# A gated mix of two linear attentions: one key-value piece issued earlier, another lock slack in the planner, one scaling on POOL, other merge orders

## The chip, the core and the metric

The kernel runs on one core of one Trainium2 chip. The core has five engines that work side by side, each through its own list of instructions in order: TensorE (PE, matrix products into PSUM; its weight loads are shown as PEld), VectorE (DVE), ScalarE (ACT), GpSimd (POOL) and SyncE (SP), which here issues the DMA transfers. They wait for each other through semaphores. The metric is the device time of one execution in microseconds; lower is better.

## The reference, cut to what matters

Two attention blocks over the same input `x` (2048 rows of 576, 32 heads of 18), mixed by a gate for each row. All data is float32.

```python
x = A_x
g = _sigmoid((x * gate_w).sum(-1, keepdims=True))
a = _A_ref(x, A_wqkv, A_wo)            # features: where(t > 0, t + 1, exp(t)) + 1e-6
b = _B_ref(x, B_wqkv, B_w_phi, B_wo)   # features: softmax(t @ w_phi) and softmax(-t @ w_phi)
return g * a + (1 - g) * b

# in each block, with feature maps pq and pk:
kv = jnp.einsum("bhsd,bhse->bhde", pk, v)
z = jnp.einsum("bhsd->bhd", pk)
num = jnp.einsum("bhqd,bhde->bhqe", pq, kv)
den = jnp.einsum("bhqd,bhd->bhq", pq, z)[..., None] + 1e-6
o = num / den                          # then (all heads side by side) @ wo
```

## The kernel before

**Three passes.** `S` is cut into 16 tiles of 128 rows, taken in eight pairs. The first pass (to about 139 us) forms keys and values of block A and sums `pk` by `v` into PSUM in key-value pieces (`kv_a`). The second (to about 273 us) does the same for block B (`kv_b`). The third makes the queries of both blocks at once, divides, transposes, multiplies by the summed key-values and by the output weights, and writes the result. Its first part, to about 350 us, is a start-up in which the first pairs come into flow; from 364 us on it repeats a block of some 34 us for each pair.

**The products.** A pair's products are one Strassen step: `strassen` makes seven products in seven units (i = 0 to 6), each a run of matmuls of 128x288 on high and low parts of an operand, into PSUM tiles named `X`, `Y` and `Z` in the code and `tr`, `pq` or `bk` in the profile. Between the units ScalarE copies a partial sum out (`keep`, shown as `row<-tr` and the like) and VectorE adds (`row<-row,pq`, `vo<-row,pq`), and TensorE may go on in that PSUM tile only when they have read it.

**The second pass.** A loop over n = 0 to 7 runs the seven units of pair n. In unit 6 it issues the key-value piece of the pair before: `kv_b(done)`, 64 matmuls of `vo` (values) by `uw`, `at` or `st` (the softmaxed keys), 19x36 each, as one piece that the planner doesn't divide. The profile records each of these float32 matmuls twice, so a piece shows as 128 records. The keys come out of `softmax_exp` (a row's maximum and minimum on VectorE, `mm`; differences; one exponential on ScalarE; the sums `ss` and their reciprocals `rs` on VectorE) and `scale_uw`, on POOL here (`uw<-uw,rs`). `steps(prep)` puts the preparation of the third pass's weights between the units: their high parts on ScalarE, the remainders on VectorE or POOL, and stores to memory (`wq<-at`, `wod<-op`).

**The third pass.** `q_units` is `strassen` with the query weights. `norm_a` and `norm_b` divide a tile by its denominators. In `norm_b` the two products of `uw` and `z_b` are on POOL and VectorE, the sums over heads (`dd<-row`) on VectorE, and then `dd<-dd,rs`, `den<-dd`, a reciprocal, `rs<-den,gate,rs` and `scale_ub` (`late<-uw,rs`). `tr_units` transposes the results (`tr<-ident,late`, `tr<-ident,row`), `num` multiplies by the key-values (`tr<-uT,kb`, `bk<-uT,kb`) and `out_units` by the output weights (`bk<-op,vo`, `bk<-op,at`). `merge` interleaves the units of these three in one list, each list with a weight and an offset: unit k of n stands at offset + weight (k + 0.5) / n.

**What sets the order.** Nothing is emitted as it is written. Every operation is recorded in a `Plan`, with a cost from `weigh` and, from `order`, a due time: for TensorE its place in the written order, for the others the due time of what needs them. `run` then simulates the engines and at each step gives an engine the operation with the earliest due time among those that could start soon. Most elementwise operations of VectorE and POOL on SBUF tiles carry `op.lock`: the planner holds that they don't overlap. `lock` is the planned end of the last such operation, and one on the other engine may start a slack before it (line 310). The order that comes out is what `emit` writes, so all instructions show line 360.

Of the kernel before, what the change touches and what calls it, by code (L numbers as in the profile page):

```python
# [15 lines left out]
ALU = mybir.AluOpType  # L16
# [131 lines left out]
class Plan:  # L148
# [128 lines left out]
    def run(self, tags):  # L277
        ops = self.ops
        for op in ops:
            op.left, op.est = len(op.deps), 0  # L280
        free = {e: 800 for e in ("PE", "ACT", "DVE", "POOL", "SP")}
        ready = {e: [] for e in free}
        slots = {tag: [0] * ts[0].bufs for tag, ts in tags.items()}
        pend = {tag: list(ts) for tag, ts in tags.items()}
        started, last, left = set(), {}, {t: t.ops for ts in tags.values() for t in ts}
        for op in ops:
            if not op.left:
                ready[op.eng].append(op)
        lock, dma, mode = 0, 0, False
        out = []  # L290
        SL = {"PE": 120, "ACT": 250, "DVE": 250, "POOL": 100, "SP": 50}
        while len(out) < len(ops):
            best = None
            for e, ops_e in ready.items():
                cand = []
                for op in ops_e:
                    s = max(free[e], op.est)
                    taken = {}
                    for t in op.tiles:
                        if t not in started:  # L300
                            free_at = sorted(slots[t.tag])
                            k = taken[t.tag] = taken.get(t.tag, -1) + 1
                            if pend[t.tag].index(t) >= len(free_at):
                                s = None
                                break
                            s = max(s, free_at[k])
                    if s is None:
                        continue
                    if op.lock:
                        s = max(s, lock - (220 if e == "POOL" else 30))  # L310
                    cand.append((s, op, 110 if e == "PE" and op.mode != mode else 0))
                if not cand:
                    continue
                first = min(s for s, _, _ in cand)
                due, _, s, op = min((op.due + 2 * turn, op.i, s + turn, op) for s, op, turn in cand if s <= first + SL[e])
                if best is None or s < best[0]:
                    best = (s, e, op)
            s, e, op = best
            ready[e].remove(op)
            for t in op.tiles:  # L320
                if t not in started:
                    started.add(t)
                    pend[t.tag].remove(t)
                    slots[t.tag].remove(min(slots[t.tag]))
            end = s + op.cost
            free[e] = end
            if op.dma:
                dma = max(s + 1000, dma) + op.dma / 370
                end = dma + 750
            elif e == "PE":  # L330
                mode = op.mode
            if op.lock:
                lock = end
            if not op.dma:
                end += op.lag
            op.key = s
            out.append(op)
            for t in op.tiles:
                left[t] -= 1
                last[t] = max(last.get(t, 0), end + self.SEM)  # L340
                if not left[t]:
                    slots[t.tag].append(last[t])
            for i in op.succ:
                o = ops[i]
                o.left -= 1
                o.est = max(o.est, end + self.SEM if o.eng != e or op.dma else end + 30 if e in ("DVE", "ACT") else free[e])
                if not o.left:
                    ready[o.eng].append(o)
        self.span = max(free.values())
        return out  # L350
# [14 lines left out]
def tile_gated_mix(ctx, tc, xT, wAk, wAv, wBv, wAq, wkT, wqT, phi, woA, woB, out):  # L365
# [382 lines left out]
    def kv_a(pend):  # L748
        with plan.piece():
            for t, f in pend:  # L750
                for gr, nh in kv_order(t):
                    p, a = side(t, gr)
                    kv_group(t, 3 * gr, nh, kv[0][64 * a:64 * a + VC * nh, 54 * p:54 * p + DH * nh],
                             f[:, 54 * gr:54 * gr + DH * nh], p == 0)

    def kv_b(pend):
        with plan.piece():
            for t, uw in pend:
                for j in range(QH):
                    for q, nh in QUADS:  # L760
                        if j < nh:
                            h = QH * q + j
                            kv_group(t, h, 1, kv[1][32 * q:32 * q + VC, 36 * j:36 * j + 36].rearrange("p (s d) -> p s d", s=2),
                                     uw[:, :, DH * h:DH * h + DH], j == 0)
# [20 lines left out]
    x = x_plain(0, raw)  # L785
# [60 lines left out]
    x = x_plain(1, raw)  # L846
# [203 lines left out]
    for n in range(NT // 2):  # L1050
        done, pend = pend, []
        if n % 2:
            lo = wk.tile([P, 2, D], F32, name="st", bufs=1) if n == 1 else area[0][:, :2 * D].rearrange("p (s n) -> p s n", s=2)
            uws = [lo, area[1][:, 896:].rearrange("p (s n) -> p s n", s=2)]
        else:
            uws = [uw_tile(), uw_tile()]
        for i, _ in enumerate(strassen(x, WB, TB, HB, two_banks, lambda: uws[0][:, 0], *b_sinks(n, uws, pend))):
            if i == 2 and n < 2:
                x_next = x_prep(n, raw, sums if n == 0 else sums[:2] + [chunks(row_tile()[:, :3 * P])])
                if n == 0:  # L1060
                    x_load_raw(1, raw)
            if i == 3 and 1 < n < NT // 2 - 1:
                x_next = x_fetch(n)
            if i == 6:
                if n:
                    kv_b(done)
                else:
                    kv_a(a_done)
            if n + i > 3:
                steps(prep)  # L1070
            if n == NT // 2 - 1 and i == 2:
                join_out()
        x = x_next
# [68 lines left out]
    def norm_b(t, uw, rs, ub, engs):  # L1142
        dd = sm.tile([P, 64], F32, name="dd")
        for s in range(2):
            zw = row_tile()[:, :D]
            engs[s].tensor_tensor(zw, uw[:, s, :], z_b[:, s], op=ALU.mult)
            V.tensor_reduce(dd[:, 32 * s:32 * s + 32], zw.rearrange("p (h d) -> p h d", d=DH),
                            op=ALU.add, axis=AX.X)
        V.tensor_tensor(dd, dd, rs, op=ALU.mult)
        den = sm.tile([P, 32], F32, name="den")  # L1150
        V.scalar_tensor_tensor(den, dd[:, :32], EPS, dd[:, 32:], op0=ALU.add, op1=ALU.add)
        V.reciprocal(den, den)
        r2 = rs.rearrange("p (s h) -> p s h", s=2)
        V.scalar_tensor_tensor(r2, den[:, None, :].to_broadcast([P, 2, 32]), gate[:, 1, at_row(t):at_row(t) + 1], r2, op0=ALU.mult, op1=ALU.mult)
        scale_ub(ub, uw, rs, engs[2])
# [115 lines left out]
    def chain(*gens):  # L1271
        for g in gens:
            yield from g
# [11 lines left out]
    for i in range(NT // 2 + 1):  # L1285
        while norms:
            norms.pop(0)()
        cur, prev = blocks[i], blocks[i - 1]
        seqs = []
        if i and i <= NT // 2:  # L1290
            prev["ot"] = num(uT, prev["at"], i >= NT // 2 - 1)
        if i + 1 < NT // 2:
            x = x_fetch(pairs[i + 1])
            if i == 0:
                load_out(3, x["dma"])
                load_out(4, x["dma"])
            if i == 1:
                for k, m in enumerate((1, 4, 6)):
                    load_out(k, x["dma"][m:m + 1])
            uws = [extra_uw, wk.tile([P, 2, D], F32, name="st", bufs=1)] if i == 0 else [uw_tile(), uw_tile()]  # L1300
            seqs.append((7, (0.4, 0) if i == 0 else (0.5, 0) if i == 1 else .7, q_units(i + 1, x, uws, row_tile)))
        ts = (2 * i + 1, 2 * i)
        if i < NT // 2:
            at = at_tile([2, 4, 256], F32R)
            cur["at"] = (at[:, 0], at[:, 1])
            seqs.append((8, (1, 0) if i == 0 else (0.7, 0.3) if i == 1 else 1, chain(*[tr_units(t, cur["at"], uT) for t in ts])))
        if i:
            seqs.append((4, (1, 0) if i == 1 else 1, chain(*[out_units(t, prev) for t in (2 * i - 1, 2 * i - 2)])))
        merge(*seqs)
    plan.emit(tc)  # L1310

# [89 lines left out]
```

## Time and profile before

| | us |
|---|---|
| three runs | 554.77, 556.88, 558.15 |
| their median | 556.88 |
| the profiled execution | 560.84 |
| its span (first to last instruction) | 559.1 |
| TensorE idle within the span, 559.1 - 544.7 | 14.4 |
| mean granted clock of TensorE | 0.994 |

The profile is of one execution, at 560.84 us somewhat above the three runs. In its rows `out<-in` are the program's tile names with the numbers left out, then the form, the type and how many (x). A time in square brackets is how long the engine stood idle ahead of the row, with what released it. "Issue" there means that the engine waited for nothing that the profile shows. The granted clock is the share of full speed at which TensorE was let run.

### The profile page before, as it was taken

Reading aid. Unit: us, or ns where it says so; the run is one execution under the profiler, and the core shown is the slowest. Engines: PE = TensorE matmul, PEld = TensorE weight load, DVE = VectorE, ACT = ScalarE, POOL = GpSimd, SP = SyncE. Lnnn points to the kernel's source line nnn. Section 1 sums busy time; section 2 is a strip of 40 time slices with the busy share of each in tenths; the row PEclk is TensorE's granted clock in tenths of the full one; section 3 lists DMA queues with packets and bytes.
Section 4 is the critical chain, followed back from the end, with each engine's and each line's share of the span. In section 5 each row is a group of like instructions: output and inputs, shape, how many; then the busy total and the mean of one; then the engine's idle time right before and its main releaser. Section 6 shows DMA issues by size and latency. Waiting matters only on the chain.

```text
span 559.1 us, 12938 instructions
## 1 busy us (share of the span) xinstructions
PE 544.7 (97%) x5233; PEld 524.7 (94%) x5233; DVE 411.5 (74%) x622; ACT 291.8 (52%) x613; POOL 252.8 (45%) x223
## 2 busy tenths in 40 slices
PE   8999998999999999999898999999999999999997
PEld 8999998999999989999898889999999999999997
DVE  5883568843698698989669999759688695976910
ACT  6665685654654545444265745445454544535521
POOL 6784396540885335354328666215243241523100
PEclk9999998999999999999899999999999999999999
DMA  8639756869578857659766921232321313100001
GB/s 283 256 130 306 263 198 244 302 232 364 186 295 290 263 197 261 200 194 333 240 189 201 366 90 51 69 106 70 105 80 59 110 54 109 68 2 23 34 32 42
DMA packets 39872, 96.38 MB, mean 172 GB/s; under 512 B 5440, under 2 KB 9024, under 8 KB 38276
## 3 DMA queue, kind: packets, MB, share of 16 engines
q1 hardware_dynamic: 39812, 95.56, 49.7%
q8 instruction: 41, 0.67, 0.5%
q14 instruction: 19, 0.16, 0.1%
HBM read 59.64 MB, written 36.70 MB: 172 GB/s over the span
## 4 chain that ended last, share of the span: by engine, by line
PE 87%; DVE 5%; ACT 2%; DMA 2%; POOL 2%; issue 2%; SPq 0%; DVEq 0%; ACTq 0%; POOLq 0%
PE pq L360 37%; PE bk L360 25%; PE tr L360 25%; ACT row L360 1%; POOL late L360 1%; DMA at<-wqT 1%; DVE at L360 1%; DVE row L360 1%; POOL row L360 1%; DVE dd L360 1%; DMA at<-xT 1%; DVE vo L360 1%; ACT op L360 0%; DMA xu<-x0x 0%; DVE st L360 0%
## 5 line engine op out<-in xcount | busy, mean ns | idle before, releaser
L360 PE MATMUL pq<-op,x 128*128 128x288 f32 (+1 forms) x636 | 105.7, 301 | 0.7 <-DVE vo L360 0.7
L360 PEld LDWEIGHTS pq<-op,x 128*128 128x128 f32 x636 | 92.1, 191 | 1.7 <-DVE vo L360 0.9
L360 PE MATMUL bk<-op,vo 128*128 128x288 f32 x480 | 70.5, 296 | 0.0
L360 PE MATMUL pq<-tail,x 128*128 128x288 f32 (+1 forms) x308 | 66.5, 300 | 0.0
L360 PEld LDWEIGHTS bk<-op,vo 128*128 128x128 f32 x480 | 65.7, 188 | 0.1
L360 POOL TENSOR_TENSOR row<-row,z_a 128x576 f32<-128x576 f32 x16 | 25.0, 1565 | 78.7 <-DVE row L360 68.4
L360 PE MATMUL pq<-op,xp 128*128 128x288 f32 (+1 forms) x336 | 53.4, 297 | 0.5 <-ACT row L360 0.5
L360 PE MATMUL bk<-op,at 128*128 128x288 f32 x288 | 51.4, 302 | 0.0
L360 ACT ACTIVATE row<-tr 128x288 f32<-128x288 f32 (+1 forms) x74 | 30.0, 407 | 38.1 <-PE tr L360 37.6
L360 PEld LDWEIGHTS pq<-tail,x 128*128 128x128 f32 x308 | 49.3, 190 | 0.6 <-DVE row L360 0.2
L360 ACT ACTIVATE row<-bk 128x288 f32<-128x288 f32 (+3 forms) x43 | 17.5, 410 | 60.5 <-PE bk L360 60.4
L360 PEld LDWEIGHTS pq<-op,xp 128*128 128x128 f32 x336 | 47.5, 188 | 0.7 <-ACT row L360 0.7
L360 ACT ACTIVATE row<-row,epsc 128x576 f32<-128x576 f32 x54 | 41.9, 776 | 7.1 <-DVE row L360 6.3
L360 DVE TENSOR_REDUCE ss<-uw 128x64 f32<-128x1152 f32 x22 | 29.6, 1347 | 20.9 <-ACT uw L360 20.8
L360 DVE TENSOR_TENSOR row<-row,pq 128x576 f32<-128x576 f32 (+1 forms) x30 | 22.4, 747 | 29.1 <-PE pq L360 14.0
L360 POOL TENSOR_TENSOR x<-at,x 128x384 fp32r<-128x384 f32 (+2 forms) x35 | 33.7, 963 | 21.8 <-ACT x L360 21.8
L360 PEld LDWEIGHTS bk<-op,at 128*128 128x128 f32 x288 | 41.8, 189 | 0.4 <-issue 0.4
L360 POOL TENSOR_TENSOR row<-row,den 128x378 f32<-128x378 f32 (+1 forms) x32 | 22.3, 715 | 31.8 <-DVE den L360 29.4
L360 PE MATMUL tr<-op,xv 128*128 128x288 f32 (+1 forms) x204 | 33.6, 302 | 0.0
L360 PE MATMUL tr<-op,xu 128*128 128x288 f32 (+1 forms) x192 | 31.1, 314 | 2.1 <-DVE row L360 2.1
L360 ACT ACTIVATE uT<-tr 118x512 f32<-118x512 f32 (+1 forms) x48 | 26.0, 560 | 13.3 <-PE tr L360 13.2
L360 ACT ACTIVATE uw<-uw 128x1152 f32<-128x1152 f32 x22 | 25.6, 1165 | 12.1 <-POOL uw L360 8.9
(206 smaller groups left out, 1251.9 us busy)
## 6 DMA issues: line engine op xcount, KB each, us to landing
xp<-s0x SPq DMA_DIRECT2D x12, 512.0 KB
at<-xT SPq DMA_DIRECT2D x18, 320.0 KB
x<-x1x SPq DMA_DIRECT2D x12, 384.0 KB
x<-s2x SPq DMA_DIRECT2D x12, 384.0 KB
s0x<-xp SPq DMA_DIRECT2D x8, 512.0 KB
out<-row SPq DMA_DIRECT2D x14, 288.0 KB
op<-wb SPq DMA_DIRECT2D x3, 1152.0 KB
wod<-op SPq DMA_DIRECT2D x3, 1152.0 KB
```

The costliest lines, as they stand in the source:

```text
L360: fn(*[a.real() if isinstance(a, View) else a for a in args], **{k: v.real() if isinstance(v, View) else v for k, v in kw.items()})
```

## The change

It has four parts. In the planner, a locked operation could be planned to start 220 ns before the end of the last one on POOL, and 30 ns on VectorE; now it is 60 ns on both. In the second pass, the key-value piece of n = 7 is issued in unit 3, not 6. In `norm_b` the product `dd<-dd,rs` is on POOL. And three pairs of weight and offset in the third pass's first two blocks are others.

```diff
                     if op.lock:
-                        s = max(s, lock - (220 if e == "POOL" else 30))
+                        s = max(s, lock - 60)
...
-            if i == 6:
-                if n:
-                    kv_b(done)
-                else:
-                    kv_a(a_done)
+            if i == 6 and not n:
+                kv_a(a_done)
+            if n and i == (6 if n < 7 else 3):
+                kv_b(done)
...
-        V.tensor_tensor(dd, dd, rs, op=ALU.mult)
+        G.tensor_tensor(dd, dd, rs, op=ALU.mult)
...
-            seqs.append((7, (0.4, 0) if i == 0 else (0.5, 0) if i == 1 else .7, q_units(i + 1, x, uws, row_tile)))
+            seqs.append((7, (0.6, 0) if i == 0 else (0.4, 0) if i == 1 else .7, q_units(i + 1, x, uws, row_tile)))
...
-            seqs.append((8, (1, 0) if i == 0 else (0.7, 0.3) if i == 1 else 1, chain(*[tr_units(t, cur["at"], uT) for t in ts])))
+            seqs.append((8, (1, 0) if i == 0 else (0.6, 0.4) if i == 1 else 1, chain(*[tr_units(t, cur["at"], uT) for t in ts])))
...
-            seqs.append((4, (1, 0) if i == 1 else 1, chain(*[out_units(t, prev) for t in (2 * i - 1, 2 * i - 2)])))
+            seqs.append((4, (0.8, 0.2) if i == 1 else 1, chain(*[out_units(t, prev) for t in (2 * i - 1, 2 * i - 2)])))
```

The set of operations is the same but for the engine of `dd<-dd,rs`; since the planner runs over the whole program, the order differs in all passes.

TensorE near the end of the second pass (n = 7), before: the piece `bk<-uw,vo` stands behind the last unit, ahead of the first product of the third pass, `tr<-op,xu`.

```order
L360 MATMUL tr<-op,xv 128x288 x6
L360 MATMUL tr<-tail,x_3216 128x288 x2
L360 MATMUL pq<-op,x_3530 128x288 x6
L360 MATMUL pq<-tail,x_3530 128x288 x2
L360 MATMUL pq<-op,x_3530 128x288 x6
L360 MATMUL pq<-tail,x_3530 128x288 x2
L360 MATMUL bk<-uw,vo 19x36 x64
L360 MATMUL tr<-op,xu 128x288 x12
```

The same place after: it stands behind the products of unit 3, ahead of unit 4.

```order
L360 MATMUL pq<-op,xp 128x288 x6
L360 MATMUL pq<-tail,x_3285 128x288 x2
L360 MATMUL pq<-op,xp 128x288 x6
L360 MATMUL bk<-uw,vo 19x36 x64
L360 MATMUL tr<-op,x_3418 128x288 x12
L360 MATMUL pq<-op,x_3352 128x288 x6
L360 MATMUL tr<-op,xv 128x288 x6
```

Between the two places lie some 45 large matmuls, so the piece moved ahead of units 4 to 6.

VectorE in the first pass, at about 90 us, before: `st<-late,st` is a remainder of the weights' preparation, `row<-tr,row` empties the accumulator `tr`.

```order
L360 TENSOR_TENSOR op<-uw,op 128x576
L360 TENSOR_TENSOR uw<-late 128x576
L360 TENSOR_TENSOR st<-late,st 128x576
L360 SCALAR_TENSOR_TENSOR row<-tr,row 128x288 x2
L360 TENSOR_TENSOR vo<-row,pq 128x32x18
```

The same place after:

```order
L360 TENSOR_TENSOR op<-uw,op 128x576
L360 TENSOR_TENSOR uw<-late 128x576
L360 SCALAR_TENSOR_TENSOR row<-tr,row 128x288 x2
L360 TENSOR_TENSOR vo<-row,pq 128x32x18
L360 TENSOR_TENSOR st<-late,st 128x576
```

The remainder now follows the emptying of `tr` and the sum into `vo`.

VectorE at the start of the third pass (about 296 to 302 us), before: `dd` and `den` are the denominators of `norm_b`.

```order
L360 TENSOR_TENSOR row<-uw,z_b 128x576
L360 TENSOR_REDUCE dd<-row 128x32 x2
L360 RECIPROCAL den<-den 128x32
L360 TENSOR_TENSOR row<-row,pq 128x576
L360 TENSOR_TENSOR dd<-dd,rs 128x64
L360 TENSOR_REDUCE dd<-row 128x32
L360 SCALAR_TENSOR_TENSOR den<-dd 128x32
```

The same place after, on VectorE, where `dd<-dd,rs` is gone and a `ss` and a `rs` stand behind the first sums:

```order
L360 TENSOR_TENSOR row<-uw,z_b 128x576
L360 RECIPROCAL den<-den 128x32
L360 TENSOR_REDUCE dd<-row 128x32
L360 RECIPROCAL rs<-ss 128x64
L360 TENSOR_REDUCE dd<-row 128x32
L360 TENSOR_REDUCE den<-row 128x32
L360 TENSOR_REDUCE ss<-uw 128x64
L360 RECIPROCAL rs<-ss 128x64
L360 SCALAR_TENSOR_TENSOR den<-dd 128x32
```

And on POOL after, where the two `dd<-dd,rs` of the first pair stand behind other products:

```order
L360 TENSOR_TENSOR row<-uw,z_b 128x576
L360 TENSOR_TENSOR row<-row,den 128x3x126
L360 TENSOR_TENSOR row<-row,den 128x198
L360 TENSOR_TENSOR dd<-dd,rs 128x64
L360 TENSOR_TENSOR row<-uw,z_b 128x576
L360 TENSOR_TENSOR late<-uw,rs 128x10x3x18 x2
L360 TENSOR_TENSOR late<-uw,rs 128x2x2x18
L360 TENSOR_TENSOR dd<-dd,rs 128x64
```

Between `dd<-row` and `den<-dd` VectorE now depends on POOL.

## The prediction

> **What bounds the kernel now.** I read the page's busy table and the shares of its chain of waits first.
>
> ```profile
> span 559.1 us, 12938 instructions
> PE 544.7 (97%) x5233; PEld 524.7 (94%) x5233; DVE 411.5 (74%) x622; ACT 291.8 (52%) x613; POOL 252.8 (45%) x223
> ```
>
> TensorE works for 544.7 of 559.1 us, and the change takes no matmul away. So what can be won is 14.4 us of idle time and whatever TensorE does at less than its full clock. The waits of TensorE by what released it came next: a reader should see that no single engine holds TensorE up, and that a line of 2.1 us has "issue" as its cause, which means that the profile shows nothing that was waited for.
>
> ```profile
> PE pq L360 <- ACT row L360: 2.2, 3, 1.3
> PE bk L360 <- issue: 2.1, 1, 2.1
> PE tr L360 <- DVE row L360: 2.1, 2, 1.9
> PE pq L360 <- DMA xu<-x0x: 1.6, 1, 1.6
> PE tr L360 <- POOL late L360: 0.8, 1, 0.8
> PE pq L360 <- DVE vo L360: 0.7, 1, 0.7
> ```
>
> The table of stretches (busy time and count of each engine, then the granted clock, DMA share and GB/s) shows the clock around the two longest of these, and how busy VectorE is where the third pass starts up (the four rows from 294 on) and in a steady block (the last).
>
> ```profile
> 90.85:93.47 2.62, 0.77 (x6) 0.53 (x5) 2.62 (x4) 1.58 (x4) 2.62 (x3) 1.00 0.06 23
> 93.47:96.88 3.41, 3.41 (x16) 3.41 (x15) 3.16 (x3) 1.13 (x3) 2.70 (x3) 0.50 0.93 287
> 270.00:273.57 3.57, 1.43 (x129) 1.25 (x124) 3.37 (x5) 1.16 (x1) 0.89 (x1) 1.00 0.35 132
> 274.38:277.79 3.41, 3.41 (x16) 3.41 (x16) 0.30 (x1) 0.82 (x2) 2.60 (x2) 0.50 0.99 340
> 294.00:308.00 14.00, 12.29 (x93) 11.83 (x92) 13.86 (x24) 7.75 (x23) 12.49 (x12) 1.00 0.64 191
> 308.00:322.00 14.00, 13.54 (x104) 11.80 (x103) 12.77 (x20) 9.71 (x22) 10.02 (x9) 1.00 0.91 365
> 322.00:336.00 14.00, 12.67 (x95) 12.29 (x94) 13.52 (x26) 5.99 (x12) 8.80 (x10) 1.00 0.28 87
> 336.00:350.00 14.00, 13.16 (x105) 12.69 (x105) 13.61 (x23) 7.79 (x17) 8.70 (x8) 1.00 0.16 55
> 364.00:398.00 34.00, 34.00 (x263) 32.72 (x262) 26.42 (x45) 16.07 (x33) 11.10 (x10) 1.00 0.26 84
> ```
>
> Two stretches of 3.41 us ran at half the granted clock, beginning 0.5 and 1.0 us after the end of a long idle time. Each does 1.7 us of full-speed work, so each costs another 1.7 us. In the steady blocks TensorE has no idle time at all, so an order that shifts VectorE or POOL there by less than their slack gives nothing. In the start-up VectorE is busy 13.86 + 12.77 + 13.52 + 13.61 = 53.8 of 56 us: there VectorE sets the pace, with TensorE waiting in turn for what VectorE releases late.
>
> **The piece issued three units earlier.**
>
> ```profile
> q8 instruction: 41, 0.67, 0.5%
> 255.09 1.40 PE L360 MATMUL bk<-at,vo 128*19 128x36 f32 x128
> 269.88 1.37 PE L360 MATMUL bk<-uw,vo 128*19 128x36 f32 x126
> 273.39 0.25 PE L360 MATMUL bk<-uw,vo 128*19 128x36 f32 x2 [2.14 <-issue]
> ```
>
> A piece is 128 recorded matmuls in 1.40 us when nothing stops it (the row at 255.09). The one that the change moves did 126 in 1.37 us, stood 2.14 us, and did the last two. All its inputs were there, since the 126 read the same tiles; what was missing, I take it, is instructions. The queue that carries instructions moved 41 packets, 0.67 MB, and TensorE has 2 x 5233 of them: about 255 to a packet, 128 matmuls with their weight loads. So a piece is as long as one packet, and spends it in 1.4 us, while packets of large matmuls (some 0.15 us each) last about 20 us. Counted along TensorE's stream, a packet's border falls after 252 of this piece's 256 instructions: the packet before it started with the piece, and the next is asked for too late. In the changed order the piece begins 90 instructions earlier in the stream, the border falls about 86 into it, as in other pieces (55 to 176) that ran through, and the next packet has several microseconds. I take the whole 2.14, and the 1.7 of the slow stretch behind it: -3.84. Bounds: 0 (the stall moves along) and -3.84.
>
> [...]
>
> Moving it has a cost too: the piece reads the products of the unit before, scaled on POOL.
>
> ```profile
> 259.25 4.28 POOL L360 TENSOR_TENSOR uw<-uw,rs 128x1152 f32<-128x1152 f32 x2
> 256.42 0.69 ACT L360 ACTIVATE at<-late 128x576 fp32r<-128x576 f32 x1
> ```
>
> That scaling ends at 263.5, and the new place, some 6 us ahead of 269.88, is at about 264: 0.5 us of margin. POOL's order there changes little, so I take 0; if the scaling is late by more than the margin, every microsecond stands in front of TensorE. ScalarE's copy `at<-late` in the second row, which waits for a store out of `at`, moves ahead of a copy that TensorE waits for (the `row<-tr` kind). Nothing here shows such a wait: bounds 0 and one of its durations each at two places, 1.4; I take 0.5, between them and nearer to the end at which the store has already landed.
>
> **The lock slack.** It changes only the planner's order. Two places in the first two passes gain.
>
> ```profile
> 90.36 0.78 ACT L360 ACTIVATE row<-row,epsc 128x576 f32<-128x576 f32 x1
> 90.59 1.97 DVE L360 TENSOR_TENSOR st<-late,st 128x576 fp32r<-128x576 f32 x1
> 92.49 0.81 DVE L360 SCALAR_TENSOR_TENSOR row<-tr,row 128x288 f32<-128x288 f32 x2
> 92.99 2.90 PE L360 MATMUL tr<-op,xu 128*128 128x290 f32 x12 [1.85 <-DVE row L360]
> 163.10 1.55 DVE L360 TENSOR_TENSOR at<-at 128x256 f32<-128x256 f32 x1
> 165.12 0.75 DVE L360 TENSOR_TENSOR vo<-row,pq 128x576 f32<-128x576 f32 x1
> 165.92 0.93 PE L360 MATMUL pq<-op,x 128*128 128x288 f32 x5 [0.68 <-DVE vo L360]
> ```
>
> At 90.59 a staging step of 1.97 us stands on VectorE ahead of `row<-tr,row`, which empties the accumulator that TensorE wants. In the changed order it stands behind, so `row<-tr,row` can start when the exponential on ScalarE ends (91.14) instead of at 92.49, 1.35 earlier, or a little before that as ScalarE's rows overlap. I take a gain of 1.45 of the 1.85, and the slow stretch that followed, 1.7. At 163.10 a remainder of 1.55 us stands ahead of `vo<-row,pq` and behind it afterwards: -0.68. Together -3.83.
>
> [...]
>
> **`den` scaling on POOL, and the merge orders.** These act in the third pass.
>
> ```profile
> L360 DVE TENSOR_TENSOR dd<-dd,rs x16: 219/285/1255, 300.2 to 527.3; 128x64 f32<-128x64 f32 x16
> 285.13 1.35 DVE L360 TENSOR_REDUCE ss<-uw 128x64 f32<-128x1152 f32 x1 [3.74 <-ACT uw L360]
> 287.06 0.55 DVE L360 RECIPROCAL rs<-ss 128x64 f32<-128x64 f32 x1
> 299.23 1.43 POOL L360 TENSOR_TENSOR row<-uw,z_b 128x576 f32<-128x576 f32 x1
> 312.59 0.31 POOL L360 TENSOR_TENSOR late<-uw,rs 128x72 f32<-128x72 f32 x1
> 325.95 0.41 ACT L360 ACTIVATE den<-den,gate 128x32 f32<-128x32 f32 x1 [3.35 <-DVE den L360]
> 326.27 0.63 ACT L360 ACTIVATE row<-pq 128x576 f32<-128x576 f32 x1
> 306.11 0.77 PE L360 MATMUL pq<-op,xu 128*128 128x288 f32 x4 [1.65 <-DMA xu<-x0x]
> 326.95 1.06 PE L360 MATMUL pq<-op,xv 128*128 128x288 f32 x6 [1.33 <-ACT row L360]
> ```
>
> Six of the 16 scalings lie in the start-up. At the median of 0.285 they relieve VectorE of 1.7 us, and at most of 6 x 1.255 = 7.5; I count 3.1, the sum of their six rows (0.22 to 1.25). A `ss` and an `rs` that VectorE did at 285 to 287, while it had idle time, now come after 294: 1.35 + 0.55 = 1.9 back. So VectorE gains 1.2 in the stretch that it paces. On POOL a scaling costs about 0.31 (its nearest row in size, 128x72), in an engine with idle time; but it is queued behind `row<-uw,z_b` (1.43), and then VectorE waits for it before `den<-dd`, with all that is queued behind.
>
> For TensorE I add up waits. Before, the start-up has 4.28: 1.65 (DMA), 0.46 of the 2.2 for ScalarE, 1.33, 0.84 (POOL `late`). After: the first goes, as other matmuls now come ahead of those on `xu`. The 1.33 falls by 0.32 to about 1.0, as ScalarE's copy now stands ahead of its `den` work. The wait for `late` stays, about 0.9. New ones: `num`'s evacuation behind a reduce on VectorE, 1.35; a `row<-row,den` on POOL behind one product, 1.4; and one wait for the scaling's round trip, 0.9, halfway between 0.31 and 1.43. Sum 5.55, so +1.3 net. Its bounds are -3 (both large waits go and nothing new comes) and +8.6 (below). In the steady blocks and the tail I cost all this at nothing: the cover is VectorE's 34.00 - 26.42 = 7.6 us of free time in each block; were it gone, a late `late` would hold up the transposes, and with them TensorE.
>
> **Sum.** -3.84 - 3.83 + 0.5 + 1.3 = -5.9 against the profiled execution's 560.84, which is 3.96 above the median of the runs, 556.88. Against the median: 551.0.
>
> **Rivals.**
> - The wait in the piece was not the packets, or comes back at another border. For it: no row shows the fetch itself. Against it: a piece of the same kind ran through at 255.09. Then 3.84 are missing: 554.8.
> - The slow stretches do not belong to the idle times, or most runs have none: the runs' spread, 554.77 to 558.15, is 3.4, two stretches' worth. For it: waits of 1.65 and 1.33 had no slow stretch behind them. Against it: both stretches follow the two longest waits. Then 3.4 are missing: 554.4.
> - The start-up gains as well: its two large waits, 2.98, go, and the new ones hide in VectorE's 1.2: -5.9 - 1.3 - 3.0 = -10.2, so 546.7. Against it: every engine's order there changes.
> - The other side: the scaling's round trip. Each of six waits on POOL behind a 1.43 product, VectorE stands, and VectorE paces that stretch: 6 x 1.43 = 8.6 in place of 1.3 gives +1.4, 558.3. It decides from (5.9 + 1.3) / 6 = 1.2 us each. Against it: the reduce behind (0.7) often fills the wait.
>
> **How the numbers follow.** About 1% either way is what a measurement of this kernel can tell from no change: 551.3 and 562.4. My forecast, 551.0, has a chance of 0.44 with a range of its own of 548.5 to 553.5; the piece not gaining 0.15, the slow stretches 0.16, the better start-up 0.13, the round trip 0.08, and 0.04 for both of the first two at once, 556.5. Faster by over 1%: 0.29 of the forecast (it sits just under the bound, with more small gains left out than costs, such as a 0.2 us wait), 0.12 of the better start-up, 0.04 of the rest: 0.45. Slower by over 1% needs a round trip of 2.1 us each: 0.05. Within: 0.50. From 546.0 to 556.5 all but the round trip and the far ends are held.
>
> **What would show it.** Right: the moved piece in one row of x128 and 1.3 to 1.4 us; no idle time over 0.6 at 91 and none at 165; granted clock 1.00 after the start; total idle near 12 us. Wrong: a piece cut in two with "issue" behind it, at any place; a slow stretch without a long idle time ahead of it; TensorE's waits in the start-up well over 5.6, with VectorE standing for POOL `dd`, or well under 3.

## The result: 548.65 us, and the profile after

The changed kernel takes 548.65 us (median of 4 runs, 547.88 to 550.29) against 557.51 (554.77 to 558.80): a ratio of 0.9851, 95% interval 0.9807 to 0.9896. The gain is clear of noise and beyond the 1% bound; 551.0 was forecast, and the range of 546.0 to 556.5 holds it.

The two profiled executions lie further apart, 560.84 and 547.88, since that of before lies above the other runs of its kernel and that of after is the lowest of its four. Their 12.96 us are what the next lines account for. First the page of the changed kernel, its head and busy table:

```profile
span 546.2 us, 12961 instructions
PE 539.3 (99%) x5233; PEld 520.1 (95%) x5233; DVE 405.0 (74%) x606; ACT 293.7 (54%) x613; POOL 254.6 (47%) x239
...
q8 instruction: 41, 0.67, 0.5%
```

TensorE's idle time fell from 14.4 to 6.9 us, and it is busy 5.4 us less with the same matmuls: the two half-speed stretches, 3.4 us, are gone, and about 1 us of the rest lies in the first 20 us (below). The last 1 us is not accounted for. The waits of TensorE:

```profile
PE bk L360 <- DVE epsc L360: 1.3, 1, 1.3
PE pq L360 <- ACT row L360: 0.9, 2, 0.7
PE pq L360 <- POOL x L360: 0.7, 1, 0.7
PE pq L360 <- DVE row L360: 0.4, 1, 0.4
PE tr L360 <- ACT uT L360: 0.2, 1, 0.2
```

The line "issue" is gone. The first line is the program's start, which before had too. The timeline of the places that the prediction named (start, duration, engine, operation); the last row but one is the moved piece:

```profile
87.98 0.78 ACT L360 ACTIVATE row<-row,epsc 128x576 f32<-128x576 f32 x1
...
88.33 0.76 DVE L360 TENSOR_TENSOR uw<-late 128x576 f32<-128x576 f32 x1
...
89.01 0.81 DVE L360 SCALAR_TENSOR_TENSOR row<-tr,row 128x288 f32<-128x288 f32 x2
...
89.79 1.77 PE L360 MATMUL tr<-op,xu 128*128 128x290 f32 x12
...
257.55 1.39 PE L360 MATMUL bk<-uw,vo 128*19 128x36 f32 x128
...
314.58 1.07 PE L360 MATMUL pq<-op,xv 128*128 128x288 f32 x6 [0.74 <-ACT row L360]
```

The emptying of `tr` now runs at 89.01, right behind the exponential, and TensorE's `tr<-op,xu` has no idle time ahead of it. The moved piece runs through, all 128 records in 1.39 us. The largest wait left in the start-up is 0.74. The next table has the time from one key-value piece of the second pass to another, from TensorE's rows, so that it holds whatever the order between them is.

| TensorE's time, us | before | after | difference |
|---|---|---|---|
| start to the first `kv_b` piece | 168.23 | 162.35 | -5.88 |
| first to eighth piece (second pass) | 116.09 | 111.83 | -4.26 |
| eighth piece to the last 1250 matmul records (start-up and first blocks) | 108.72 | 105.94 | -2.78 |
| the last 1250 records (steady blocks and tail) | 162.48 | 162.44 | -0.04 |

The sum is -12.96. Within the first row, by equal counts of matmuls, 0.68 was won by the 15th microsecond, 0.76 between 61 and 81, 3.5 at the wait at 91, and 0.93 at that at 165. The 0.68 is 1.4 won less 0.7 lost to a new wait for POOL (`POOL x` in the list above), and the 1.4 is not the change's: TensorE ran its first matmuls at about half rate, before until 11.5 us and after until 8.2. The same six matmuls, before and then after:

```profile
8.57 1.65 PE L360 MATMUL pq<-op,xu 128*128 128x290 f32 x6
...
8.27 0.98 PE L360 MATMUL pq<-op,xu 128*128 128x290 f32 x6
```

The kernel of experiment 11, which has the order of before on these engines, took 0.97 for them. Its first row is 164.61, with the wait at 91 in it (1.67) and no half-speed stretch behind: some 3.6 of the 5.88 come and go between executions of one order.

### The profile page after: what moved, and what is told of

Read it like the earlier page. It is cut to its first block, busy times and chain, and to the rows that moved or that the text cites. A ratio compares the mean times of both kernels' runs of the same rounds, so it can differ in the third digit from the quotient of the medians.

```text
span 546.2 us, 12961 instructions
## 1 busy us (share of the span) xinstructions
PE 539.3 (99%) x5233; PEld 520.1 (95%) x5233; DVE 405.0 (74%) x606; ACT 293.7 (54%) x613; POOL 254.6 (47%) x239
## 4 chain that ended last, share of the span: by engine, by line
PE 91%; DVE 3%; DMA 2%; POOL 2%; ACT 1%; issue 0%; SPq 0%; POOLq 0%
PE pq L360 37%; PE tr L360 28%; PE bk L360 26%; DMA x<-x3x 1%; DVE row L360 1%; DMA at<-xT 1%; POOL kb L360 1%; DVE den L360 1%; DVE ss L360 0%; POOL late L360 0%; ACT row L360 0%; SPq L360 0%; DVE dd L360 0%; POOL x L360 0%; DVE mm L360 0%
## 5 line engine op out<-in xcount | busy, mean ns | idle before, releaser
L360 PE MATMUL pq<-op,x 128*128 128x288 f32 (+1 forms) x636 | 104.0, 298 | 0.0
L360 PEld LDWEIGHTS pq<-op,x 128*128 128x128 f32 x636 | 90.7, 188 | 1.0 <-issue 0.4
L360 POOL TENSOR_TENSOR x<-at,x 128x384 fp32r<-128x384 f32 (+2 forms) x35 | 32.4, 925 | 21.9 <-ACT x L360 19.3
L360 DVE TENSOR_TENSOR vo<-row,pq 128x576 f32<-128x576 f32 x28 | 21.0, 749 | 12.0 <-ACT row L360 11.5
L360 DVE TENSOR_TENSOR at<-at 128x256 f32<-128x256 f32 (+1 forms) x38 | 23.9, 656 | 7.9 <-DMA at<-xT 7.7
```

Source lines behind the costliest of these rows:

```text
L360: fn(*[a.real() if isinstance(a, View) else a for a in args], **{k: v.real() if isinstance(v, View) else v for k, v in kw.items()})
```

## The experiments

Twelve kernels were run, and with each group of them the kernel before was timed anew on the same chip. A result is the ratio of the times to before, with its 95% interval; below 1 is faster.

**1. Padding in the kernel before.** The first warm-up matmul is repeated, when the planned order is written out.

```diff
         order = self.order()
+        first = next(op for op in order if op.eng == "PE")
+        first.calls = first.calls * 21
```

> The kernel before in its own order, with the first warm-up matmul issued 20 more times: 40 more instructions at the head of TensorE's stream, nothing else. If the stall in the key-value piece at 271 us is a late packet of instructions (a packet is asked for when the one before the last begins to be used up, and a packet that holds almost only a piece lasts 1.4 us), the borders now fall 40 instructions earlier in the program, the packet around that piece also holds some 20 large matmuls (3 us), and both the 2.14 us and the slow stretch behind it are gone: the piece is one row of x128, no piece elsewhere stalls, time about 3.5 us under the kernel before. If the place or its inputs cause it, the piece still stands 2.1 us behind its 126th record and the time is that of before, within 1 us.

Measured: 1.0103 [1.0066, 1.0140], slower. Most of it is the warm-up itself: the first piece starts at 172.10 instead of 168.23. In the timeline of TensorE the stall has not gone. It has moved within the piece:

```profile
273.78 1.16 PE L362 MATMUL bk<-uw,vo 128*19 128x36 f32 x106
276.61 0.45 PE L362 MATMUL bk<-uw,vo 128*19 128x36 f32 x22 [1.67 <-issue]
```

It came after the 106th record instead of the 126th: 40 instructions earlier, exactly the 40 that were put in (a record is two). So it sits on a border counted in instructions, and neither the place nor the inputs can do that. But the 3 us of large matmuls within the packet didn't cover it. The expectation was right on where and wrong on how long.

**2. Padding in the changed kernel**, the same with 46 in place of 21.

> The changed kernel in its own order, with the first warm-up matmul issued 45 more times (90 instructions). If packets of instructions decide, the count along the stream says that five of the eight pieces of the second pass now stall, where the changed kernel has none: the first by about 0.6 us, the second 1.5, the fourth 1.4, the seventh 2 and the last 0.5, 6 us in all, with slow stretches of 1.7 behind some of them; with up to 5 us for the warm-up itself at the start, 8 to 15 us over the changed kernel. If packets don't matter, no piece stalls and only the start is longer, 0 to 5 us.

Measured: 1.0064 [1.0037, 1.0091] of before, so about 12 us over the changed kernel; some 8 of them stand ahead of the first piece (170.17 against 162.35). Three pieces stalled, of five expected:

```profile
192.38 0.25 PE L362 MATMUL bk<-at,vo 128*19 128x36 f32 x5 [1.48 <-issue]
...
233.32 1.20 PE L362 MATMUL tr<-op,xu 128*128 128x288 f32 x7 [0.87 <-issue]
```

These are the second piece and, just behind it, the fourth; the third stall is 1.90 in the seventh, the one moved by the change. In each the stall is at the record that the count gives (123 of the second piece, five large matmuls behind the fourth). So the changed kernel can be made to stall by nothing but a shift of its stream. The two pieces counted to lose about 0.5 didn't.

**3 and 4. The moved piece alone, and the change without it.** The edit of the second; that of the first is its reverse, on the kernel before.

```diff
-            if i == 6 and not n:
-                kv_a(a_done)
-            if n and i == (6 if n < 7 else 3):
-                kv_b(done)
+            if i == 6:
+                if n:
+                    kv_b(done)
+                else:
+                    kv_a(a_done)
```

> The kernel before with only the piece of n = 7 in unit 3. By the prediction's step: -3.8 us, since the moved piece lies well inside a packet. But counted along the stream of this kernel, the piece of n = 6 has moved too and now begins 5 instructions behind a border: if packets decide, that piece stalls by some 2.1 us in its place, and the gain is nothing (within 1 us). If the place near the end of the second pass were the cause, no piece stalls and 3.8 us are won.

> The changed kernel with the piece of n = 7 back in unit 6. By packets it begins 5 instructions behind a border again: a stall of about 2.1 us in that piece and probably a slow stretch of 1.7 behind it, so 2 to 4 us over the changed kernel. If the other parts of the change had removed the stall, the time is that of the changed kernel.

Measured: the piece moved alone gives 0.9937 [0.9901, 0.9972], about 3.5 us, as the prediction had it and against the count; the change without it gives 0.9880 [0.9844, 0.9916], where the whole gives 0.9851, a difference within the intervals. In the profile of the first the piece of n = 6, 5 instructions behind a border, runs through at 251.13, and 0.40 us of "issue" remain behind that of n = 7:

```profile
251.13 1.40 PE L360 MATMUL bk<-at,vo 128*19 128x36 f32 x128
...
264.98 1.38 PE L360 MATMUL bk<-uw,vo 128*19 128x36 f32 x128
...
270.79 0.54 PE L360 MATMUL pq<-tail,x 128*128 128x288 f32 x2 [0.40 <-issue]
```

And that of the second:

```profile
263.54 1.35 PE L360 MATMUL bk<-uw,vo 128*19 128x36 f32 x125
265.43 0.25 PE L360 MATMUL bk<-uw,vo 128*19 128x36 f32 x3 [0.54 <-issue]
```

The border falls where it is counted (record 125), but the stall is 0.54, not 2.1. So every stall stands at a border, but the border doesn't set its size. What does is read from the records of the instruction queue: when the packet landed, and when TensorE went on (us; the first column has the experiment's number).

```
kernel            piece at  stops after  idle  packet lands  goes on  between
before              269.88          126  2.14        271.81   273.39     1.6
1 padded before     273.78          106  1.67        275.12   276.61     1.5
2 padded after      189.57          123  1.48        190.86   192.38     1.5
2 padded after      230.19          133  0.87        231.71   233.32     1.6
2 padded after      269.85          126  1.90        271.85   273.12     1.3
4 without the piece 263.54          125  0.54        263.90   265.43     1.5
5 slack alone       264.05          125  0.10        264.06   265.50     1.4
6 scaling alone     268.45          126  0.80        269.17   270.62     1.5
7 merge alone       267.56          126  1.88        269.46   270.81     1.4
11 later loads      266.23          126  3.17        269.48   270.77     1.3
12 slack, POOL only 263.86          125  3.06        266.63   268.27     1.6
```

In all eleven, TensorE goes on 1.3 to 1.6 us after its packet has landed. So it does at the three other idle times with "issue" as their cause, which lie among large matmuls: 0.17 in the first padded kernel, 0.40 with the moved piece alone, 0.83 with the old slack (experiment 10). Counted from the start, with weight loads, matmul records and TensorE's semaphore and drain instructions, all fourteen lie 192 or 193 instructions behind a multiple of 256. In the profile of the kernel before 256 is also the step of the packets: from the first of the 41 to the last 10219 of these instructions started, 255 to a packet. There, by the same count, each packet began to move with TensorE 22 to 291 instructions ahead of its border (from 364 us on 251 to 290), the one of the stall with 22. That the stall is the instruction supply is shown by this and by the two paddings. Its length, 0.10 to 3.17 us in the table, is how late the packet comes.

**5 and 12. The slack alone, and that of POOL alone.** The edit of 12; that of 5 is the first of the change.

```diff
-                        s = max(s, lock - (220 if e == "POOL" else 30))
+                        s = max(s, lock - (60 if e == "POOL" else 30))
```

> The kernel before with only the lock slack of 60 ns. My step: the waits at 91 (1.85) and 165 (0.68) and the slow stretch behind the first go, -4.2 us, the stall in the piece of n = 7 stays (it begins 5 instructions behind a border). Theory that the start-up's gain (2.8 us between 290 and 345 in the changed kernel, where I had expected a loss of 1.3) also comes from the planner's order by the slack: then another -2 to -3 there. Rival: the start-up's gain comes from the merge orders or from the scaling on POOL, then the start-up here is within 1 us of before.

> The kernel before with the slack of POOL alone at 60 ns (VectorE stays at 30). If planning POOL less early (220 to 60) makes the gain of the slack, the wait at 91 is gone and the time is within 1.5 us of the kernel with both at 60 (549.2). If VectorE's slack (30 to 60) is what moves the remainder behind the emptying of tr, the wait at 91 stays and the time is 554 to 557. Chance either way: the planner's order depends on small differences of its costs.

Measured: 0.9879 [0.9831, 0.9927] for both engines at 60, 549.19 us, and 0.9889 [0.9840, 0.9939] for POOL alone. The slack by itself is nearly the whole change. The waits at 91 and 165 are gone in both, so POOL's part of the slack is enough to remove them. With both at 60 the second pass takes 111.94 us, against 111.83 in the changed kernel, although the piece of n = 7 still stands in unit 6 on a border: its packet came early enough. With POOL alone the packet came late, and that piece shows the second longest of these stalls:

```profile
263.86 1.35 PE L360 MATMUL bk<-uw,vo 128*19 128x36 f32 x125
268.27 0.25 PE L360 MATMUL bk<-uw,vo 128*19 128x36 f32 x3 [3.06 <-issue]
```

The start-up with the slack alone is 106.78 against 108.72 before: a gain of 1.9, just under the 2 to 3 that I had expected if the slack carried it.

**6 and 9. The scaling on POOL alone, and the change without it.** The edit of 6; 9 is its reverse.

```diff
-        V.tensor_tensor(dd, dd, rs, op=ALU.mult)
+        G.tensor_tensor(dd, dd, rs, op=ALU.mult)
```

> The kernel before with only dd<-dd,rs on POOL. If VectorE's relief in the start-up makes the gain there, -1 to -3 us between 290 and 345; if the round trip through POOL costs, +1 to +8 in the same stretch. The steady blocks and the first two passes: no difference in either case, so the stall at 271 and the wait at 91 stay.

> The changed kernel with dd<-dd,rs back on VectorE. If the scaling on POOL gives the start-up's gain (VectorE relieved by 3 us), the start-up is 1 to 3 us longer than in the changed kernel; if it costs a round trip, it is shorter; if it is hidden, within 0.5 us. No difference ahead of 285 us.

Measured: alone 1.0034 [1.0002, 1.0066], slower by 0.3%; without it 0.9885 [0.9835, 0.9934]. The loss is where neither theory looked, in the steady blocks. TensorE's waits for VectorE in the kernel with the scaling alone (total, times, longest, in us):

```profile
PE tr L360 <- DVE vo L360: 1.6, 4, 0.4
```

And one of them in its timeline:

```profile
377.42 1.39 DVE L360 SCALAR_TENSOR_TENSOR den<-dd 128x32 f32<-128x32 f32 x1 [0.21 <-POOL dd L360]
...
382.09 1.28 DVE L360 TENSOR_TENSOR vo<-tr,vo 128x512 fp32r<-128x512 f32 x2
...
382.92 0.63 PE L360 MATMUL tr<-ident,row 128*128 128x128 f32 x4 [0.44 <-DVE vo L360]
```

VectorE waits 0.21 for POOL's `dd` and is then late with `vo<-tr,vo`, which empties the accumulator that TensorE wants: about 0.4 in each of four blocks, and the last 1250 records take 164.22 instead of 162.48. In the changed kernel they take 162.44. There the scaling itself is cheap, and VectorE hardly waits:

```profile
L360 POOL TENSOR_TENSOR dd<-dd,rs x16: 321/324/768, 288.5 to 513.9; 128x64 f32<-128x64 f32 x16
...
  DVE den L360: 0.2, 1
```

(min, median and max in ns; the second row is who waited for it, in us.) Taking it out of the changed kernel costs 0.5 us in the start-up, in one profile each.

**7 and 8. The merge orders alone, and the change without them.** The edit of 7, the first of its three lines; 8 is its reverse.

```diff
-            seqs.append((7, (0.4, 0) if i == 0 else (0.5, 0) if i == 1 else .7, q_units(i + 1, x, uws, row_tile)))
+            seqs.append((7, (0.6, 0) if i == 0 else (0.4, 0) if i == 1 else .7, q_units(i + 1, x, uws, row_tile)))
...
```

> The kernel before with only the new weights and offsets of merge. If the order of the start-up's units makes the gain there, the 1.65 us wait for xu and the 1.33 us wait for ScalarE's copy go and the stretch from 290 to 345 is 2 to 3 us shorter; otherwise it is within 1 us. The first two passes as before: waits at 91, 165 and the stall at 271 stay.

> The changed kernel with the old weights and offsets of merge. If the merge orders give the start-up's gain, the stretch from 290 to 345 us takes 2 to 3 us more than in the changed kernel; if the slack or the scaling does, within 1 us. Ahead of 285 us nothing differs.

Measured: alone 1.0003 [0.9960, 1.0047], no difference; without them 0.9870 [0.9828, 0.9912]. The start-up alone with the new merge takes 110.22, which is 1.5 more than before, and in the changed kernel without it 108.97, which is 3.0 more. Of these 3.0 a wait for a load is the largest piece:

```profile
277.79 1.04 PE L360 MATMUL tr<-op,xv 128*128 128x288 f32 x6 [1.74 <-DMA op<-wq]
```

That wait lies ahead of anything that `merge` places, so it is not shown that the weights caused it. In the medians (550.89 against 548.65) the loss is smaller than in the profile.

**10. The change with the old slack.**

```diff
-                        s = max(s, lock - 60)
+                        s = max(s, lock - (220 if e == "POOL" else 30))
```

> The changed kernel with the old lock slack (220 ns on POOL, 30 on VectorE). The waits at 91 (1.85) and 165 (0.68) come back with a slow stretch, +4 us. By packets, the piece of n = 6 now begins 5 instructions behind a border and stalls 2.1 us in place of that of n = 7, with a slow stretch, another 2 to 4. In the start-up, +0 to +3. Together 6 to 10 us over the changed kernel, near the kernel before.

Measured: 0.9993 [0.9957, 1.0028]. With three of its four parts in place the change gains nothing. The start-up takes 108.00, the last 1250 records 164.17 (the same four waits as with the scaling alone), and 0.83 us of "issue" stand behind the piece of n = 7. The wait at 91 did not come back, though it stays with each of the three parts alone: it belongs to the one order that the planner found in the kernel before, not to the slack of 220 as such. That at 165 did, with 0.68.

**11. Later loads.** The three loads `op<-wq` are planned behind the piece of n = 7; the orders of TensorE, VectorE, ScalarE and POOL are those of before.

```diff
-            plan.first = x.get("dma", ())
+            plan.first = [*x.get("dma", ()), *piece_at[-1:]]
...
+        piece_at.append(len(plan.ops) - 1)
```

> The kernel before, with the three loads of stored query weights (op<-wq, 1152 KB each) held until the key-value piece of n = 7 has run; the order on TensorE, VectorE, ScalarE and POOL is that of before, and the border still falls after 252 of the piece's 256 instructions. If the packet of instructions comes late because it stands behind these transfers (in every run so far it moved only when the DMA share had fallen from 1.0), it now comes 2 to 5 us earlier and the stall in that piece is 0 to 0.5 us, against 0.8 to 2.1 in the runs with this order; the loads then come later and may hold up the third pass's fifth unit by 0 to 3 us. If the packet is asked for only at the border and takes its 3.5 us whatever else moves, the stall stays at about 2.

Measured: 1.0045 [1.0008, 1.0082], and the stall became longer:

```profile
262.96 2.43 SPq L360 DMA_DIRECT2D op<-wq  x3
```

That was SyncE's queue; and TensorE:

```profile
266.23 1.37 PE L360 MATMUL bk<-uw,vo 128*19 128x36 f32 x126
270.77 0.24 PE L360 MATMUL bk<-uw,vo 128*19 128x36 f32 x2 [3.17 <-issue]
```

Both expectations missed. The dependence acted in the planner alone: the loads were issued from 262.96, ahead of the piece and not behind it, and so moved beside it; in the kernel before the third of them was issued at 273.56. The packet started 2.3 us after the piece, instead of 1.0, in a stretch in which the 16 DMA engines were full (a DMA share of 0.97 and more). That fits a packet that waits behind data transfers, as they now stood beside it. But with the moved piece alone two packets moved at shares of 0.94 and 0.96, so a full queue does not always hold a packet up. What delays a packet stays open.

## Why the prediction was right, and where not

- **What bounds the kernel: right.** Idle time and half-speed stretches were what was won in the profiled pair; the steady blocks, with no idle time, gave 0.04.
- **The wait at 91 and its slow stretch, -1.45 and -1.7: right for the profiled pair, a little small.** 3.5 came, as the wait went entirely; the 0.4 that I had left of it did not appear. Of the 1.7 a typical execution has less, see the slow stretches.
- **The wait at 165, -0.68: right,** 0.93 came over the stretch around it. Another 1.4 in the first pass (0.76 about a wait of 0.25 at 75, and the 0.68 at the start) were not in the sum.
- **The piece, -3.84: the size right, the attribution wrong.** Second pass and piece gave -4.26 where -3.84 + 0.5 was forecast. Alone the move gains about 3.5 us. But in the step "the next packet has several microseconds" a border's distance from the piece was taken to settle it. The packet's arrival settles it as much: with the slack alone the piece stands on the border in unit 6 and loses 0.10. So beside the slack the move is worth 0.1 us in the second pass (111.83 against 111.94), or 0.6 against the change without the move (112.44). The 55 to 176 of other pieces mix two counts: they are how far behind a border those pieces begin. The border falls 80 to 202 instructions into them, and the 86 is still among these.
- **The first rival,** that the wait is no matter of instructions, is refuted by the paddings. The fourteen stalls cost 0.1 to 3.2 us each.
- **The slow stretches: right in the profile, and wrong for a typical execution.** They belong to idle times (last section), which refutes the first half of the second rival. Its other half holds: most executions have none. A stretch of 3.41 us at 0.50 in a span of 559.1 takes 0.003 off the mean granted clock, so the clock of an execution counts them. Of 65 executions of the kernel before that were timed beside the experiments, 37 had 0.999 or 1.000, 19 had 0.996 or 0.997, and 9 had 0.993 or 0.994, with medians of 555.35, 557.62 and 560.02 us. The profiled execution, with two stretches and 0.994, is of the rarest kind. There 3.4 could be won; on average it is 1.0, by an estimate from these counts (37 stretches of 1.7 us in 65 executions).
- **The start-up, +1.3: wrong.** It gave -2.8, near the -3.0 of the third rival. The step that failed is the adding up of waits: the 1.35, 1.4 and 0.9 that I read from the order as new waits of TensorE, and 0.9 for `late`, did not reach it. Only the wait for ScalarE's copy did, 0.74 where 1.0 was forecast, with 0.15, 0.35 and 0.24 at three other places. Together they are 1.48, where 5.55 was added up; waits "well under 3" there were named as a sign of being wrong. No part carries the gain alone: against before, the piece gives -1.7 there, the slack -1.9, the scaling -1.0 and the merge +1.5. What in the order makes the gain stays open.
- **The scaling on POOL hidden in the steady blocks: right for the whole change, wrong for the part.** The cover I named, 7.6 us of VectorE's free time per block, is a sum over the block and says nothing of one late instruction; with the old slack it cost 0.4 per block.
- **The round trip,** the rival on the other side, is absent: VectorE waited 0.2 us for `dd` in all.

Of the other signs named, the moved piece in one row, no idle time at 91 and 165, and a clock of 1.00 came; total idle time is 6.9 us, not near 12.

That 551.0 came within 2.4 us of the result is in part luck. In the profiled pair the sum missed by 7.1 (12.96 against 5.9), 4.1 of it in the start-up. Against the medians, which lie 8.9 apart, it missed by less, as two errors met. The -5.9 held 3.4 for half-speed stretches, which most executions don't have, and +1.3 for a start-up that gained 2.8 in the profiles.

## What to carry to other kernels

A stall of TensorE with "issue" as its cause, inside a run of many short matmuls, is to be checked against the count of instructions: the one here came earlier by exactly the 40 instructions put in front (a weight load and a matmul to a record), so it was late supply. Moving the run cured it only as long as nothing else shifted the stream: with 90 instructions put in front, the changed kernel stalled in three places, by 0.87 to 1.90 us. Where a planner sets the order, try its constants one by one before the hand-made moves: here one slack brought 1.2% of the 1.5%, and the other three parts together without it nothing (0.9993, though the moved piece alone gave 0.6%). A part that costs on its own can be free in another order, so parts are taken out of the whole as well as tried alone.

## What the runs showed of the hardware

The half-speed stretches of a profile lay on a grid of 3.41 us: in the kernel before the two start 180.91 us apart, 53 times 3.413, and in the kernel with the merge orders alone 34.13, ten times. In these profiles a stretch followed where TensorE's idle time within one cell of the grid (a step of 3.41 us) was more than about half of it. In the profiles of all fourteen kernels, after the first 20 us and up to the cell of TensorE's last matmul, six cells had 1.85 us or more (1.85, 1.86, 1.88, 2.08, 2.14 and 3.14) and each was followed by one; of the cells with less, the next ones (1.84, 1.78, 1.74 and 1.67) were not, and one exception, 1.48 in the padded changed kernel, was. The cell of the last matmul had 1.87 in the kernel before and was not followed by one. The bound is read off these same cells, so it is no more than that. One cell and the next, in the kernel with the merge orders alone (busy times of PE, PEld, DVE, ACT and POOL, then the granted clock):

```profile
302.16:305.57 3.41, 1.33 (x11) 1.36 (x12) 3.34 (x9) 0.90 (x2) 2.07 (x5) 1.00 0.87 293
305.57:308.98 3.41, 3.41 (x17) 3.39 (x16) 1.49 (x3) 2.82 (x8) 3.33 (x4) 0.50 0.98 340
```

The same kernel waited 1.84 us at 90, split over two cells, and no stretch followed. So of two waits of near 1.9 us here one cost 1.84, and the other, 1.85 within one cell, some 3.6 with its stretch. The grid also fits the spread of the kernel before, which has two waits of that size: 552.5 to 560.3 in 20 executions beside the first experiments, ten of them at a clock of 0.999 or 1.000 (median 555.3) and three at 0.993 (559.0). The changed kernel, without such waits, ran from 547.9 to 550.3 in four, at 0.999 and 1.000.
